# Loading the first piece of w_out as two transfers, of 120 and of 8 partitions, in a packed-attention and feed-forward kernel

## The chip, the cores and the metric

The kernel runs on one core of a Trainium2 chip. The metric is the device time of one execution in microseconds (us). Before the change the median of three runs is 711.92 us (711.51 to 712.25).

## The reference

Each of 8 batches has 8 heads of 576 tokens and 64 dimensions. A set of 32 packed queries `p` attends to `k` and `v`, and the queries `q` attend to what comes out; the heads of a token, side by side, are the 512 inputs of a feed-forward layer with 2048 hidden units.

```
p_packed = sm_attn(p, k, v)
out = sm_attn(q, p_packed, p_packed)
x = attn_out.transpose(0, 2, 1, 3).reshape(B * S, H * D)
h = x @ w_in
g = np.maximum(h, 0.0) + alpha * np.minimum(h, 0.0)
return (g @ w_out)
```

`w_in` (512 x 2048) and `w_out` (2048 x 512) come as 64-bit floats and are turned into 32-bit ones on the chip.

## The kernel before

The second attention is not multiplied out: the kernel multiplies the packed result with `w_in` first (`packed_w`, tiles `pw`), and TensorE (PE) then forms the hidden units of a tile of tokens from the attention weights and `pw` (`first`, lines 764 to 812) and from them the output (`second`, lines 878 to 921, and `row_second`). A tile has 288 or 256 tokens, a step of the main loop one tile and one of 16 blocks of hidden units. The first four tiles are swept over a part of the hidden units at a time, so that the weights can arrive and be converted meanwhile.

Before the main loop lies a start of some 25 us in which batch 0 goes through its whole attention. Its order is a string of letters, `go("inaaauoiaaaIaboaiiaa0abooavbawaOIx")` (line 990): `a` and `b` take a step of the attention of batch 0 and 1, `i` and `o` load the next piece of `w_in` and `w_out`, `I` and `O` convert one, `u`, `v`, `w`, `x` issue spare matmuls (`keep_busy`). The instructions of each engine run in the order that a scheduler settled when the kernel was built.

`w_out` is loaded in eight pieces (`w_out_load`, line 202). Piece `g` is 256 rows of 512 64-bit numbers, two rows for each of 128 partitions, 1 MB in one DMA. All loads go through `load` (line 181), and nearly all are issued by SyncE (SP) at line 189, in the order in which the program asks for them.

The framework gives each DMA one of eight semaphores in turn, `DMAHW0` to `DMAHW7`. Before SP issues a DMA it waits until the DMA that had the same semaphore before, the eighth before it, has landed. So at most eight are under way. Whoever reads the data waits for that semaphore too.

The first piece (tile `wraw0`, in the profile `wraw<-in_w_out`) is converted by `to_half` (line 153): ScalarE (ACT) takes the magnitude of the upper words (line 151, to `wo_whole`), then the sign and the lower words (lines 175 and 176, to `rest`); VectorE (DVE) limits and shifts the magnitude (lines 166 and 169) and adds `rest` (line 177). Right behind it ACT converts the second piece of `w_in` (`wraw5`, again lines 151 and 131), on which DVE waits with line 132. The first product with `w_out` is at line 896.

Of the kernel before, what the change touches and what calls it, by code (L numbers as in the profile page):

```python
# [27 lines left out]
def pack_attention_ffn_kernel(  # L28
# [19 lines left out]
    B, NP, P, S = qT.shape  # L48
# [132 lines left out]
    def load(out, in_, eng=None):  # L181

        if eng is not None:
            other.append(eng.dma_start(out=out, in_=in_))
            return
        with ExitStack() as behind:
            if queue:
                behind.enter_context(tc.issue_after(queue[-1].ins))
            ins = nc.sync.dma_start(out=out, in_=in_)
        if written:  # L190
            queue[:] = [ins]

    first_half, begun = [], []
    last_mm, queue, written, raws, tail, whole, w0, other = [], [], [True], {}, {}, [], [], []
# [6 lines left out]

    def w_out_load(g):
        raws["o", g] = const.tile([P, 2, 512], U64, name=f"wraw{g}", tag=f"wo{g}")
        load(raws["o", g], w_out[2 * g * P : 2 * (g + 1) * P, :].rearrange("(a p) d -> p a d", p=P))

    def w_out_convert(g):
        if g < QF:
# [747 lines left out]
    def go(what):  # L955


        for ch in what:
            if ch in BUSY:
                keep_busy(BUSY[ch], values[BEHIND[ch]] if ch in BEHIND else None)  # L960
            elif ch == "n":
                load(al, alpha)
                nc.gpsimd.tensor_scalar(
                    out=nal, in0=al, scalar1=-1.0, scalar2=1.0, op0=ALU.mult, op1=ALU.add
                )
            elif ch in "ab":
                next(a0 if ch == "a" else a1, None)
            elif ch in counts:
                n = counts[ch]
                counts[ch] += 1  # L970
                if ch == "0":
                    if n < 2:
                        packed_w(0, 0, (n,))
                    else:
                        packed_w(0, n - 1)
                elif ch == "1":
                    packed_w(1, n, (None,) if n else (0, 1))
                else:
                    with ExitStack() as behind:
                        for ins in tail.values() if ch != "A" else []:  # L980
                            behind.enter_context(tc.issue_after(ins.ins))
                        {
                            "i": w_in_load, "I": w_in_convert, "o": w_out_load,
                            "O": w_out_convert, "S": w_out_late_split, "H": late_a, "A": w_out_begin,
                        }[ch](n)
# [142 lines left out]
```

## Time and profile before

| | before |
|---|---|
| median of 3 runs | 711.92 us (711.51 to 712.25) |
| the profiled execution: time / span | 712.62 us / 710.8 us |
| busy: PE, DVE, ACT | 98%, 67%, 50% of the span |
| DMA | 85.36 MB, mean 120 GB/s |
| DMA from 0 to 60 us | 21.12 MB, mean 352 GB/s |

The span runs from the first to the last instruction; the execution's time has some 2 us around it. The profile names a group of instructions by its line, engine, operation and tiles (written <- read). All times inside an execution are us from the start of the span.

### The profile page before, as it was taken

Reading aid. Unit: us, or ns where it says so; the run is one execution under the profiler, and the core shown is the slowest. Engines: PE = TensorE matmul, PEld = TensorE weight load, DVE = VectorE, ACT = ScalarE, POOL = GpSimd, SP = SyncE. Lnnn points to the kernel's source line nnn. Section 1 sums busy time; section 2 is a strip of 40 time slices with the busy share of each in tenths; the row PEclk is TensorE's granted clock in tenths of the full one; section 3 lists DMA queues with packets and bytes.
Section 4 is the critical chain, followed back from the end, with each engine's and each line's share of the span. In section 5 each row is a group of like instructions: output and inputs, shape, how many; then the busy total and the mean of one; then the engine's idle time right before and its main releaser. Section 6 shows DMA issues by size and latency. Waiting matters only on the chain.

```text
span 710.8 us, 14597 instructions
## 1 busy us (share of the span) xinstructions
PE 695.5 (98%) x5600; PEld 599.2 (84%) x5600; DVE 474.3 (67%) x1067; ACT 358.1 (50%) x846; POOL 33.0 (5%) x128
## 2 busy tenths in 40 slices
PE   6899999999999999999999999999999999999997
PEld 3578998899898888888878888888887888798897
DVE  4999888865796568656773567846694456964443
ACT  3796788944355535444443454545353333533232
POOL 1001200001001200001000010001000000000000
PEclk9899999999999999999999999999999999999999
DMA  9996474133534422452323423334314203010100
GB/s 312 385 342 244 129 261 151 60 104 122 155 117 156 135 59 99 148 156 73 126 47 118 156 68 127 125 100 120 97 59 152 66 7 95 25 30 1 30 16 30
DMA packets 77188, 85.36 MB, mean 120 GB/s; under 512 B 34880, under 2 KB 57920, under 8 KB 77120
## 3 DMA queue, kind: packets, MB, share of 16 engines
q1 hardware_dynamic: 76480, 83.89, 36.4%
q8 instruction: 44, 0.72, 0.4%
q10 hardware_dynamic: 640, 0.56, 0.2%
q14 instruction: 24, 0.20, 0.1%
HBM read 70.79 MB, written 13.63 MB: 119 GB/s over the span
## 4 chain that ended last, share of the span: by engine, by line
PE 92%; DVE 3%; DMA 2%; ACT 2%; issue 0%; SPq 0%; DVEq 0%
PE acc L832 40%; PE ps_h L780 9%; PE ps_h L782 9%; PE ps_h L781 9%; PE acc L899 5%; PE acc L900 5%; PE acc L901 5%; PE ps_m L375 4%; PE ps_j L375 3%; PE acc L896 2%; PE acc L375 2%; DMA wraw<-in_w_out 1%; DMA xtwo<-in_kT 1%; PE ps_h L774 1%; PE spare L286 0%
## 5 line engine op out<-in xcount | busy, mean ns | idle before, releaser
L832 PE MATMUL acc<-wo,gh 128*128 128x512 f32 x704 | 200.1, 398 | 0.0
L787 ACT ACTIVATE neg<-ps_h 128x256 f32<-128x256 f32 (+2 forms) x256 | 105.4, 412 | 164.4 <-PE ps_h L782 157.8
L801 DVE SCALAR_TENSOR_TENSOR neg<-neg,nal,ps_h 128x256 f32<-128x256 f32 (+1 forms) x248 | 119.6, 483 | 77.1 <-ACT neg L787 76.6
L811 ACT CAST gh<-neg 128x256 fp32r<-128x256 f32 (+1 forms) x248 | 101.7, 411 | 111.3 <-DVE neg L801 110.0
L780 PE MATMUL ps_h<-a_h,pw 128*128 128x256 f32 (+2 forms) x496 | 146.4, 295 | 0.8 <-DVE neg L801 0.8
L782 PE MATMUL ps_h<-a_h,pw 128*128 128x256 f32 (+2 forms) x496 | 146.6, 296 | 0.0
L781 PE MATMUL ps_h<-a_l,pw 128*128 128x256 f32 (+2 forms) x496 | 146.5, 295 | 0.0
L812 DVE TENSOR_TENSOR gl<-neg,gh 128x256 fp32r<-128x256 f32 (+1 forms) x248 | 104.4, 425 | 61.5 <-ACT gh L811 59.8
L832 PEld LDWEIGHTS acc<-wo,gh 128*128 128x128 f32 x704 | 126.7, 195 | 21.9 <-issue 4.2
L832 PE MATMUL acc<-wo,gl 128*128 128x512 f32 x352 | 115.5, 394 | 0.0
L780 PEld LDWEIGHTS ps_h<-a_h,pw 128*128 128x128 f32 x496 | 93.5, 188 | 7.6 <-DVE neg L801 1.3
L781 PEld LDWEIGHTS ps_h<-a_l,pw 128*128 128x128 f32 x496 | 93.4, 188 | 7.2
L782 PEld LDWEIGHTS ps_h<-a_h,pw 128*128 128x128 f32 x496 | 93.5, 189 | 0.1
L900 PE MATMUL acc<-gh,wo 128*128 128x288 f32 (+1 forms) x280 | 79.7, 293 | 0.5 <-DVE wo L237 0.5
L832 PEld LDWEIGHTS acc<-wo,gl 128*128 128x128 f32 x352 | 68.7, 195 | 13.5
L899 PE MATMUL acc<-gh,wo 128*128 128x288 f32 (+1 forms) x280 | 80.0, 296 | 0.0
L901 PE MATMUL acc<-gl,wo 128*128 128x288 f32 (+1 forms) x280 | 69.8, 293 | 0.0
L899 PEld LDWEIGHTS acc<-gh,wo 128*128 128x128 f32 x280 | 52.6, 189 | 5.0 <-ACT pw L730 3.4
L900 PEld LDWEIGHTS acc<-gh,wo 128*128 128x128 f32 x280 | 52.8, 189 | 0.7 <-DVE wo L237 0.7
L794 DVE SCALAR_TENSOR_TENSOR rest<-neg,nal,ps_h 128x64 f32<-128x64 f32 x96 | 26.6, 277 | 40.1 <-ACT neg L787 40.1
L901 PEld LDWEIGHTS acc<-gl,wo 128*128 128x128 f32 x280 | 48.6, 188 | 0.7 <-issue 0.5
L832 PE MATMUL acc<-wo,rparts 128*128 128x512 f32 x144 | 35.3, 397 | 0.0
(157 smaller groups left out, 690.1 us busy)
## 6 DMA issues: line engine op xcount, KB each, us to landing
w<-w_whole SPq DMA_DIRECT2D x48, 512.0 KB, 5.8
wraw<-in_w_in SPq DMA_DIRECT2D x8, 1024.0 KB, 10.9
wraw<-in_w_out SPq DMA_DIRECT2D x8, 1024.0 KB, 6.8
xraw<-in_kT SPq DMA_DIRECT2D x28, 288.0 KB, 4.5
xraw<-in_qT SPq DMA_DIRECT2D x28, 288.0 KB, 4.6
vraw<-in_v SPq DMA_DIRECT2D x96, 64.0 KB, 2.1
outT<-out SPq DMA_DIRECT2D x44, 128.0 KB, 2.2
w_whole<-w SPq DMA_DIRECT2D x6, 512.0 KB, 7.6
```

The costliest lines, as they stand in the source:

```text
L375: mm = nc.tensor.matmul(out, lhs, rhs, start=start, stop=stop)
L780: nc.tensor.matmul(x, w[:, 0, i], a_h[:, i], start=(i == 0), stop=False)
L781: nc.tensor.matmul(x, w[:, 0, i], a_l[:, i], start=False, stop=False)
L782: mm = nc.tensor.matmul(x, w[:, 1, i], a_h[:, i], start=False, stop=(i == 1))
L787: marks[:] = [mm, nc.scalar.activation(out=neg, in_=x, func=AF.Relu, scale=-1.0)]
L801: nc.vector.scalar_tensor_tensor(out=g, in0=neg, scalar=nal[:, f : f + 1], in1=x, op0=ALU.mult, op1=ALU.add)
L811: late[:] = [nc.scalar.copy(out=gh, in_=g)]
L812: nc.vector.tensor_tensor(out=gl, in0=g, in1=fv(gh), op=ALU.subtract)
L832: mm = nc.tensor.matmul(ps, g, wo_t[f][:, part_], start=(f == 0 and i == 0), stop=(f == NF - 1 and i == 2))
L899: nc.tensor.matmul(ps, wo_t[f][:, 0, os_], gh, start=begin, stop=False)
L900: nc.tensor.matmul(ps, wo_t[f][:, 1, os_], gh, start=False, stop=False)
L901: mm = nc.tensor.matmul(ps, wo_t[f][:, 0, os_], gl, start=False, stop=end)
```

## The change

`w_out_load` issues the load of piece 0 as two DMAs into the same tile: partitions 0 to 119 and partitions 120 to 127. The other seven pieces stay one DMA each.

```diff
     def w_out_load(g):
         raws["o", g] = const.tile([P, 2, 512], U64, name=f"wraw{g}", tag=f"wo{g}")
-        load(raws["o", g], w_out[2 * g * P : 2 * (g + 1) * P, :].rearrange("(a p) d -> p a d", p=P))
+        src = w_out[2 * g * P : 2 * (g + 1) * P, :].rearrange("(a p) d -> p a d", p=P)
+        for part_ in ((slice(0, 120), slice(120, P)) if g == 0 else (slice(0, P),)):
+            load(raws["o", g][part_], src[part_])
```

SP has one DMA more, and every later DMA gets the next semaphore of the eight. On SP, from the last two loads of `q` for batch 0 (`xtwo`) on, there stands before the change (`wraw4`, `wraw5`, `wraw6` are pieces of `w_in`, `xraw` is `k` of batch 1):

```order
L189 DMA xtwo_130<-in_qT 128x2x288 [waits DMAHW5_49]
L189 DMA xtwo_131<-in_qT 128x2x288 [waits DMAHW6_49]
L189 DMA wraw0_178<-in_w_out 128x2x512 [waits DMAHW7_49,PE_49]
L189 DMA wraw5_180<-in_w_in 128x4x256 [waits DMAHW0_49]
L189 DMA praw_226<-in_pT 128x128 [waits DMAHW1_49]
L189 DMA xraw_228<-in_kT 128x576 [waits DMAHW2_49]
L189 DMA xraw_230<-in_kT 128x576 [waits DMAHW3_49]
L189 DMA xraw_232<-in_kT 128x576 [waits DMAHW4_49]
L189 DMA xraw_234<-in_kT 128x576 [waits DMAHW5_49]
L189 DMA wraw1_236<-in_w_out 128x2x512 [waits DMAHW6_49,PE_49]
L189 DMA wraw6_283<-in_w_in 128x2x512 [waits DMAHW7_49]
L189 DMA wraw4_285<-in_w_in 128x2x512 [waits DMAHW0_49,DVE_49,Activation_49]
```

and with the change, at the same place of SP:

```order
L189 DMA xtwo_131<-in_qT 128x2x288 [waits DMAHW6_49]
L189 DMA wraw0_178<-in_w_out 120x2x512 [waits DMAHW7_49,PE_49]
L189 DMA wraw0_178<-in_w_out 8x2x512 [waits DMAHW0_49]
L189 DMA wraw5_181<-in_w_in 128x4x256 [waits DMAHW1_49]
L189 DMA praw_227<-in_pT 128x128 [waits DMAHW2_49]
L189 DMA xraw_229<-in_kT 128x576 [waits DMAHW3_49]
L189 DMA xraw_231<-in_kT 128x576 [waits DMAHW4_49]
L189 DMA xraw_233<-in_kT 128x576 [waits DMAHW5_49]
L189 DMA xraw_235<-in_kT 128x576 [waits DMAHW6_49]
L189 DMA wraw1_237<-in_w_out 128x2x512 [waits DMAHW7_49,PE_49]
L189 DMA wraw6_284<-in_w_in 128x2x512 [waits DMAHW0_49]
L189 DMA wraw4_286<-in_w_in 128x2x512 [waits DMAHW1_49,DVE_49,Activation_49]
```

From `wraw5` to the second piece of `w_out` (`wraw1`), seven loads now wait for a DMA that is one later in the program than before: `wraw1` waited for the last load of `q` and now waits for the 120 partitions of `wraw0`. From `wraw6` on each load waits for the DMA it waited for before (where that was `wraw0`, for the 8 partitions).

On ACT, at the conversion of the first piece, before:

```order
L551 ACTIVATE t1_291<-t1_291 128x576 [waits DVE_49]
L151 ACTIVATE wo_whole_376<-wraw0_178 128x1024 [waits DMAHW7_49]
L175 ACTIVATE rest_377<-wraw0_178,tiny_106 128x1024 [waits Activation_49]
L176 ACTIVATE rest_377<-wraw0_178 128x1024 [waits Activation_49]
L151 ACTIVATE w_384<-wraw5_180 128x1024 [waits DMAHW0_49]
```

and with the change (lines behind 205 are two higher):

```order
L553 ACTIVATE t1_292<-t1_292 128x576 [waits DVE_49]
L151 ACTIVATE wo_whole_377<-wraw0_178 128x1024 [waits DMAHW7_49,DMAHW0_49]
L175 ACTIVATE rest_378<-wraw0_178,tiny_106 128x1024 [waits Activation_49]
L176 ACTIVATE rest_378<-wraw0_178 128x1024 [waits Activation_49]
L151 ACTIVATE w_385<-wraw5_181 128x1024 [waits DMAHW1_49]
```

The instruction at line 151 waits for both DMAs; the order of ACT, DVE and PE is as it was.

## Rows read from the trace of the kernel before

**Rows 1.** The page: busy time of the engines, share of the span, instructions.

```profile
PE   695.5 (98%) x5600; PEld 599.2 (84%) x5600; DVE 474.3 (67%) x1067; ACT 358.1 (50%) x846; POOL 33.0 (5%) x128
```

**Rows 2.** Waits for a DMA, whole span: total, times, longest (us).

```profile
PE acc L375 <- DMA xtwo<-in_kT: 4.6, 2, 4.2
...
ACT wo_whole L151 <- DMA wraw<-in_w_out: 0.5, 1, 0.5
```

**Rows 3.** The chain that ended last, 0 to 40 us: start, length, work.

```profile
11.70 8.98 DMA wraw<-in_w_out
...
20.70 1.12 ACT wo_whole L151
...
25.34 0.69 DVE w L132
```

**Rows 4.** Timeline of ACT: start, length, instruction, idle before and its releaser.

```profile
19.55 0.68 ACT L551 ACTIVATE t<-t 128x576 f32<-128x576 f32 x1 [0.82 <-DVE t L541]
20.70 1.12 ACT L151 ACTIVATE wo_whole<-wraw 128x1024 f32<-128x1024 f32 x1 [0.47 <-DMA wraw<-in_w_out]
...
29.32 1.15 ACT L151 ACTIVATE wo_whole<-wraw 128x1024 f32<-128x1024 f32 x1
```

**Rows 5.** Waits of DVE from 20 to 60 us, all of them.

```profile
DVE w L132 <- ACT w L151: 0.9, 1, 0.9
```

**Rows 6.** DMA issues from 0 to 11.69 us: count, KB each, median us to landing.

```profile
xtwo<-in_qT SPq DMA_DIRECT2D x4, 288.0 KB, 7.5
wraw<-in_w_in SPq DMA_DIRECT2D x1, 1024.0 KB, 7.3
vtwo<-in_v SPq DMA_DIRECT2D x2, 512.0 KB, 8.6
xtwo<-in_kT SPq DMA_DIRECT2D x3, 288.0 KB, 4.5
xtwo<-in_kT ACTq DMA_DIRECT2D x1, 288.0 KB, 4.1
vtwo<-in_v SPq DMA_DIRECT2D x2, 64.0 KB, 8.2
praw<-in_pT ACTq DMA_DIRECT2D x1, 64.0 KB, 2.7
```

**Rows 7.** Stretches: length, busy time (instructions) of each engine, granted clock, DMA share, GB/s.

```profile
0.00:4.00 4.00, 0.00 (x0) 0.00 (x0) 0.00 (x0) 1.49 (x2) 1.80 (x13) 1.00 0.48 154
4.00:8.00 4.00, 3.44 (x32) 0.65 (x32) 0.82 (x2) 0.00 (x0) 0.00 (x0) 1.00 1.06 372
8.00:12.00 4.00, 4.00 (x27) 3.95 (x24) 2.12 (x9) 2.78 (x9) 0.20 (x1) 1.00 1.03 330
12.00:16.00 4.00, 2.15 (x84) 1.47 (x82) 3.75 (x7) 1.85 (x6) 0.00 (x0) 1.00 1.09 348
16.00:18.00 2.00, 1.94 (x48) 0.81 (x48) 1.97 (x4) 0.00 (x1) 0.00 (x0) 1.00 1.04 415
18.00:20.00 2.00, 1.23 (x10) 1.19 (x10) 1.97 (x4) 1.11 (x3) 0.00 (x0) 1.00 1.02 382
...
24.00:28.00 4.00, 4.00 (x24) 1.97 (x23) 3.10 (x5) 2.91 (x5) 0.00 (x0) 0.53 1.03 409
```

**Rows 8.** DMA queues, 14 to 18 us: packets, MB, share of 16 engines.

```profile
q8 instruction: 1, 0.02, 1.6%
```

**Rows 9.** DMA issued from 16.8 to 17 us: the second piece of w_out.

```profile
wraw<-in_w_out SPq DMA_DIRECT2D x1, 1024.0 KB, 12.3
```

**Rows 10.** Timeline of SP: start, length of the issue.

```profile
2.29 0.47 SPq L189 DMA_DIRECT2D wraw<-in_w_in  x1
...
12.11 0.47 SPq L189 DMA_DIRECT2D wraw<-in_w_in  x1
13.62 0.34 SPq L189 DMA_DIRECT2D praw<-in_pT  x1
...
16.87 0.38 SPq L189 DMA_DIRECT2D wraw<-in_w_out  x1
```

## The prediction

> **What bounds the kernel now.** I began with the page: PE is busy for 695.5 of the 710.8 us [rows 1], so at most 15.3 us of the span can be won anywhere without taking work from PE. The change touches a load, so the second view was the waits for a DMA over the whole span [rows 2]. The reader is to see how few there are: PE waits for the first `k` at the very start, and the only wait for `w_out` is one of 0.5 us on ACT, at line 151. Third came the chain that ended last [rows 3]: it runs through the first piece of `w_out`, from its issue at 11.70 to line 151 at 20.70, on ACT to the magnitude of the next piece, and from there to DVE at 25.34. The timeline of ACT [rows 4] gives the wait its size: line 551 ended at 19.55 + 0.68 = 20.23, and ACT then sat idle for 0.47 us. Last, the waits of DVE [rows 5]: between 20 and 60 us it waits once worth listing, 0.9 us, for the magnitude that ACT makes. So what ACT loses at 20.2 DVE loses at 25.3, and after that DVE is the engine that PE waits for.
>
> **Why that load lands late.** The bytes asked for up to the first `w_out` piece are the issues of [rows 6] (4 x 288 + 1024 + 2 x 512 + 4 x 288 + 2 x 64 + 64 = 4544 KB, the 8 KB of `alpha` left out) and its own 1024 KB: 5568 KB, or 5.70 MB. What moved, by stretch [rows 7]: 4 x (154 + 372 + 330 + 348) GB/s = 4.82 MB by 16 us, 0.83 MB more by 18, and 382 GB/s from there. So 5.70 MB had moved at 18.1 us, and the piece landed at 20.7. If the 16 DMA engines were level, the time between would be the tail of a transfer. For the first `w_in` piece the same sum gives 2.29 MB (2240 KB), reached at 8.6, with its landing at 2.29 + 7.3 = 9.6 [rows 6, 10]: a tail of 1.0. For `w_out` it is 2.5, so some 1.5 us are something else. One thing in these microseconds is out of the ordinary: a single instruction packet of 16 KB that took 1.6% of 16 engines over 4 us, 0.016 x 16 x 4 = 1.02 us [rows 8]. Being one packet, it occupied one engine. My reading is that one DMA engine falls a good 1 us behind, and that a transfer dealt over all 16 waits for it.
>
> **The change, part by part.**
> - *The split.* Dealt evenly, each of 16 engines carries 8 partitions of the piece, 64 KB. At 382 / 16 = 23.9 GB/s [rows 7] a partition of 8 KB costs an engine 0.34 us. How 120 partitions are dealt no row shows, since all loads here have a multiple of 16. I take 15 engines with 8 each, because 120 is 15 x 8, and one partition each on eight engines for the rest: one engine then carries nothing, eight carry nine.
> - *If the late engine is the one left out*, the piece lands at 18.1 + 1.0 + 0.34 = 19.5, before ACT is free at 20.23. Line 151 starts at 20.25, 0.45 us earlier. More cannot come, since ACT's earlier work is not moved. DVE's 0.9 us shrinks by the same 0.45, and everything behind it in the start moves up by that. What is late next is ACT itself.
> - *If it is not left out*, it is among the other 15 and the landing stays at 20.7, or is 0.34 later if it is one of the eight with a ninth partition.
> - *One more issue on SP*, 0.4 us like the others (0.34 to 0.47 [rows 10]), and seven loads that wait for a DMA one place later. The `w_in` piece goes from 12.11 to 13.6, where the DMA behind it stood, whose wait it takes over [rows 10]; the second `w_out` piece from 16.87 to the landing of the first, 19.5 to 21.0. Cost: nothing, as long as work lies ahead of them. Asked for by then are 5.70 + 1024 + 64 + 4 x 288 KB = 8.0 MB, moved by 20.7 are 5.64 + 2.7 x 0.38 = 6.7. The 1.3 MB between are 3.4 us of DMA time, more than the shortest time to landing in the start, 2.7 us [rows 6]. The second piece used to land at 16.87 + 12.3 = 29.2 [rows 9] and is read at 29.32 [rows 4]; with this cover it still does. If the cover were gone, the gap of some 2 us would pass on to it, and ACT at 29.3 would be late by as much.
> - *A second semaphore on line 151*: no row prices it on ACT; between nothing and 0.1 us, I take nothing.
>
> Sum: 0.45 us less, in the profiled execution 712.62 - 0.45 = 712.17. The median lies 0.70 below that execution, so 711.92 - 0.45 = **711.5 us**. That is 0.06%, and about 0.2% (1.4 us) is what a measurement of this kernel can tell from no change: the verdict should be "same".
>
> [...]
>
> **The rivals.**
> - *The late engine is not left out*: 711.9, or 712.3 if it takes a ninth partition. For it: no row numbers the engines. [...]
> - *Fewer engines, slower.* 120 is no multiple of 16, and if it is dealt to 8 engines, each carries 15 partitions instead of 8: 7 x 0.34 = 2.4 us more, landing at 23.1. ACT, DVE and all behind them are late by 2.4: 714.3. It turns the change over once the late engine carries more than its 8 partitions of now, and can be measured from four more on (4 x 0.34 = 1.4 us). Nothing in the trace speaks for it.
> [...]
>
> **How the numbers follow.** Late engine left out, 711.5: 0.45, a choice and not a count, since blind odds would be far lower and a fixed place at the end of the row is what lifts them. Not left out: 0.28 for 712.3 and 0.13 for 711.9. Fewer engines: 0.05. Clock better 0.05, worse 0.04. The runs before spread by -0.4 and +0.3, so 711.5 to 712.3 with that spread is 711.1 to 712.6; with a little for the clock on either side the range is 710.8 to 712.9, which leaves out the fewer engines and most of the clock cases. Below 710.5 lies the better clock: faster 0.05. Above 713.3 lie fewer engines and the worse clock: slower 0.09. Same: 0.86.
>
> **What would show it.** Right: two issues of `w_out` near 11.7 and 12.1, the second piece of `w_out` issued at 19 to 20 instead of 16.87, ACT's line 151 at 20.25 with no wait for a DMA, DVE's wait at line 132 near 0.45, the start of DVE's and PE's later work 0.4 to 0.45 earlier. Wrong: line 151 at 20.7 or 21.0 with the second `w_out` issue just before it (the late engine still carries the piece), or at 23 (fewer engines); a wait of ACT at its second line 151 near 29.3 (the cover was gone); the granted clock low in a stretch where it was full.

## The result and the profile after

| | before | after |
|---|---|---|
| median of 6 runs each, side by side | 712.17 us (711.51 to 712.95) | 716.05 us (715.33 to 717.3) |
| the profiled execution: time / span | 712.62 / 710.8 us | 715.46 / 713.6 us |
| ratio, 95% interval | | 1.0053 [1.0042, 1.0063] |

The change costs 3.9 us by the medians and 2.8 in the two profiled executions, of which the one after lies 0.6 below its median and the one before 0.45 above its own. The prediction was 711.5, within [710.8, 712.9]: wrong, and on the wrong side.

Lines behind 205 are two higher than in the rows of before. The page, first the busy time of the engines, which answers to [rows 1], and its row of the loads' DMA queue:

```profile
PE 697.2 (98%) x5600; PEld 598.9 (84%) x5600; DVE 474.9 (67%) x1067; ACT 357.9 (50%) x846; POOL 32.8 (5%) x128
...
q1 hardware_dynamic: 76487, 83.89, 36.9%
```

No engine does more work to speak of. The queue has 76,487 packets for the same 83.89 MB. Before it had 76,480, so there are 7 more, to which x2_64_64 below comes back:

```profile
q1 hardware_dynamic: 76480, 83.89, 36.4%
```

The chain that ended last, which answers to [rows 3], start, length, work:

```profile
11.84 11.47 DMA wraw<-in_w_out
...
23.37 9.30 DMA wraw<-in_w_out
32.66 0.02 issue
32.69 0.02 ACT wo_whole L151
```

The first piece now lands at 11.84 + 11.47 = 23.3, where it landed at 20.7; behind it the chain runs through a second load of `w_out`. The timeline of ACT, which answers to [rows 4] (start, length, instruction, idle before and its releaser):

```profile
20.29 0.69 ACT L553 ACTIVATE t<-t 128x576 f32<-128x576 f32 x1
23.39 1.15 ACT L151 ACTIVATE wo_whole<-wraw 128x1024 f32<-128x1024 f32 x1 [2.41 <-DMA wraw<-in_w_out]
...
32.69 1.16 ACT L151 ACTIVATE wo_whole<-wraw 128x1024 f32<-128x1024 f32 x1 [0.48 <-DMA wraw<-in_w_out]
```

ACT waits 2.41 us for the piece where it waited 0.47, and its line 151 starts at 23.39, 2.69 later. DVE inherits that (waits of DVE from 20 to 60 us, against [rows 5]):

```profile
DVE w L132 <- ACT w L151: 2.1, 1, 2.1
```

DVE's line 132 moved from 25.34 to 28.04 (2.70), its transpose of batch 0's last attention weights (line 568, now 570) from 37.08 to 39.79 (2.71), and the span grew by 2.8. So the loss is complete at line 151 and travels through unchanged. The chain runs through the second load as well, but DVE has no idle time left between 28.04 and 39.79, so the wait for that load adds nothing. Where it arises is seen in the stretches, with the columns of [rows 7]; first the kernel after:

```profile
16.00:20.00 4.00, 2.60 (x51) 1.34 (x52) 3.93 (x7) 0.36 (x2) 0.00 (x0) 1.00 1.04 201
20.00:24.00 4.00, 2.61 (x21) 2.23 (x21) 2.89 (x6) 1.59 (x4) 0.00 (x0) 1.00 1.02 240
24.00:28.00 4.00, 3.28 (x12) 1.45 (x12) 1.39 (x2) 3.97 (x5) 0.00 (x0) 0.52 1.06 388
28.00:32.00 4.00, 4.00 (x19) 1.90 (x15) 3.96 (x6) 2.24 (x6) 0.00 (x0) 0.63 1.03 406
```

and the same stretches before:

```profile
16.00:20.00 4.00, 3.16 (x58) 2.00 (x58) 3.93 (x7) 1.12 (x4) 0.00 (x0) 1.00 1.03 398
20.00:24.00 4.00, 2.58 (x13) 2.42 (x12) 3.83 (x8) 3.50 (x4) 0.00 (x0) 0.61 1.06 385
```

This is the main reading. The DMA engines are as busy as before (share 1.04 against 1.03; the share adds up the time of all packets, and can come out above 1), and move half as much: 201 GB/s against 398. They lack nothing to do; what they do takes longer. The granted clock is no cause: before it is 0.61 and 0.53 from 20 to 28 us [rows 7 for the second], after it is 0.52 and 0.63 from 24 to 32 (the last two rows of after), the same low stretch some 4 us later; and x2_64_64 below, with a granted clock of 1.00 from 16 to 32 us, is as slow. One microsecond of it by packets, 16 to 17 us, after:

```profile
DMA packets 55, 0.19 MB, mean 186 GB/s; under 512 B 0, under 2 KB 10, under 8 KB 55
## 3 DMA queue, kind: packets, MB, share of 16 engines
q1 hardware_dynamic: 55, 0.19, 105.4%
```

and before:

```profile
DMA packets 117, 0.44 MB, mean 436 GB/s; under 512 B 4, under 2 KB 13, under 8 KB 117
## 3 DMA queue, kind: packets, MB, share of 16 engines
q1 hardware_dynamic: 117, 0.44, 108.4%
```

The share times 16 engines and 1 us, divided by the packets, is the mean time of one: 1.054 x 16 / 55 = 0.31 us after, 1.084 x 16 / 117 = 0.15 before. A packet takes twice as long.

### The profile page after: what moved, and what is told of

Read it like the earlier page. It is cut to its first block, busy times and chain, and to the rows that moved or that the text cites. A ratio compares the mean times of both kernels' runs of the same rounds, so it can differ in the third digit from the quotient of the medians.

```text
span 713.6 us, 14600 instructions
## 1 busy us (share of the span) xinstructions
PE 697.2 (98%) x5600; PEld 598.9 (84%) x5600; DVE 474.9 (67%) x1067; ACT 357.9 (50%) x846; POOL 32.8 (5%) x128
## 2 busy tenths in 40 slices
DMA packets 77195, 85.36 MB, mean 120 GB/s; under 512 B 34887, under 2 KB 57927, under 8 KB 77127
## 3 DMA queue, kind: packets, MB, share of 16 engines
q1 hardware_dynamic: 76487, 83.89, 36.9%
## 4 chain that ended last, share of the span: by engine, by line
PE 89%; DMA 5%; DVE 3%; ACT 2%; issue 1%; SPq 0%; DVEq 0%
PE acc L834 40%; PE ps_h L782 9%; PE ps_h L784 9%; PE ps_h L783 9%; PE acc L901 5%; PE acc L902 5%; PE acc L903 5%; PE ps_m L377 3%; DMA wraw<-in_w_out 3%; PE ps_j L377 3%; PE acc L377 2%; DMA wraw<-in_w_in 1%; DMA xtwo<-in_kT 1%; DVE wo L239 0%; PE spare L288 0%
```

## The experiments

Theories: **A**, a transfer over part of the partitions is slow by itself, whatever else is under way: its packets take longer, and by how much depends on which partitions it covers. Why it should be so, no run shows. Against it stood: one more DMA (its issue, its semaphore, the later waits of SP); that only 15 engines carry the large part; that the rows are read from memory in a worse order; that other traffic of the start is in the way.

| run | first piece cut into | time us | ratio [95%] | GB/s, 16 to 20 us | ACT L151 at |
|---|---|---|---|---|---|
| before | whole | 712.17 | 1 | 398 | 20.70 |
| after | 120 + 8 partitions | 716.05 | 1.0053 [1.0042, 1.0063] | 201 | 23.39 |
| x1_two_rows | two rows, 128 partitions each | 712.29 | 0.9994 [0.9985, 1.0003] | 395 | 20.23 |
| x2_64_64 | 64 + 64 partitions | 716.39 | 1.0049 [1.0034, 1.0063] | 210 | 23.89 |
| x3_112_16 | 112 + 16 partitions | 715.09 | 1.003 [1.0017, 1.0043] | 252 | 23.45 |
| x4_source_order | 120 + 8, other source rows | 717.6 | 1.0059 [1.0042, 1.0076] | 193 | 26.17 |
| y2_columns | 480 + 32 columns, 128 partitions | 712.39 | 1.0001 [0.9991, 1.001] | 381 | 20.58 |
| y3_96_32 | 96 + 32 partitions | 714.07 | 1.0026 [1.0016, 1.0035] | 225 | 21.81 |
| z3_mid_first | 32..95, 0..31, 96..127 | 714.17 | 1.0017 [1.0007, 1.0027] | 256 | 20.95 |

Each ratio is to runs of the kernel before on the same chip, with medians of 712.97 (x runs), 712.26 (y), 712.68 (z1, z2) and 712.81 (z3).

**Two transfers, all partitions** (x1_two_rows). The piece's two rows are the two DMAs, 512 KB each (this cut and those of y2 and z3 are shown against the changed kernel):

```diff
-        for part_ in ((slice(0, 120), slice(120, P)) if g == 0 else (slice(0, P),)):
-            load(raws["o", g][part_], src[part_])
+        for part_ in ((slice(0, 1), slice(1, 2)) if g == 0 else (slice(0, 2),)):
+            load(raws["o", g][:, part_], src[:, part_])
```

> The first piece of w_out is loaded as two transfers of all 128 partitions, one per row of a partition (512 KB each), so there is one DMA more and the same shift of the waits on SP as with 120 and 8 partitions, but both are dealt as a whole transfer is. [...] Rival C (one DMA more, the later waits and the second semaphore on ACT cost the time): 715 to 716, the second piece of w_out issued after 20 and landing after 32.

712.29 us, ratio 0.9994 [0.9985, 1.0003]. The DMA from 16 to 17 us, with the columns above:

```profile
DMA packets 128, 0.42 MB, mean 419 GB/s; under 512 B 15, under 2 KB 30, under 8 KB 128
```

and the timeline of ACT:

```profile
20.23 1.11 ACT L151 ACTIVATE wo_whole<-wraw 128x1024 f32<-128x1024 f32 x1
...
28.50 1.15 ACT L151 ACTIVATE wo_whole<-wraw 128x1024 f32<-128x1024 f32 x1 [0.24 <-DMA wraw<-in_w_out]
```

The second DMA, its issue on SP, the second semaphore at line 151 and the seven loads that wait one place later are all here as in the change, and cost nothing that can be measured. The second `w_out` piece was issued at 18.47, and rival C falls. What costs is how the cut goes.

**Half the partitions each** (x2_64_64).

```diff
-        for part_ in ((slice(0, 120), slice(120, P)) if g == 0 else (slice(0, P),)):
+        for part_ in ((slice(0, 64), slice(64, P)) if g == 0 else (slice(0, P),)):
```

> The first piece is loaded as partitions 0 to 63 and 64 to 127. [...] Theory B (15 engines are what is slow): 712 us and 400 GB/s. Rival C: 715 to 716 with 400 GB/s. [...]

716.39 us, as slow as the change with its 716.05; theory B (15 engines) falls. The page's row of the queue, and the stretches:

```profile
q1 hardware_dynamic: 76496, 83.89, 36.8%
```

```profile
16.00:20.00 4.00, 2.16 (x41) 0.79 (x45) 3.78 (x6) 0.27 (x1) 0.00 (x0) 1.00 1.05 210
20.00:24.00 4.00, 2.68 (x35) 2.06 (x21) 3.13 (x7) 1.34 (x4) 0.00 (x0) 1.00 1.01 235
```

76,496 packets are 16 more than before, and all 16 are under 512 B (34,896 such packets against 34,880). x1, whose two DMAs keep all 128 partitions, shows the same two numbers. In the kernel before, SP's 376 DMAs leave 6,016 packets of 4 bytes in the trace, 16 for each DMA, and the page counts 16 engines. The trace numbers no engine; if each engine that takes part leaves one such packet, which is my estimate from these counts, the halves run on as many engines as whole transfers do, and are slow all the same: the engine left idle is not the cause. By the same estimate the change's 7 more, all under 512 B too (34,887), are 15 + 8 in place of 16, that is 15 engines for 120 partitions and 8 for 8.

**112 + 16 and 96 + 32** (x3_112_16, y3_96_32), cut in the same way, with 112 and 96 in place of 64.

> The first piece is loaded as 112 and 16 partitions, 7 and 1 for each of 16 engines. [...] Theory B: 712 us and 400 GB/s. Rival C: 715 to 716.

715.09 us, 252 GB/s from 16 to 20 us, line 151 at 23.45. The queue has 76,496 packets as in x1 and x2, so by that count all 16 engines take part again, and it is still slow.

> The first piece is loaded as 96 and 32 partitions, 6 and 2 for each of 16 engines. Theory A: both transfers cover the partitions unevenly, 250 to 300 GB/s from 16 to 20 us, ACT's line 151 at 22 to 23.5 and 714 to 715.5 us. Theory B (only an odd number of engines is slow): 712 us.

714.07 us, as theory A had it, and 76,496 packets again, but with 225 GB/s from 16 to 20 us (250 to 300 were expected) and 355 from 20 to 24, and with line 151 at 21.81 (22 to 23.5). All four of these cuts across partitions are slower than the whole, and by different amounts; why 96 costs less than 64 was not worked out.

**Another source order** (x4_source_order): 120 + 8 partitions, with the rows of `w_out` read so that a partition's two rows lie side by side in memory. This permutes the rows of `w_out` in the first piece, so the product is with other rows.

```diff
-        src = w_out[2 * g * P : 2 * (g + 1) * P, :].rearrange("(a p) d -> p a d", p=P)
+        src = w_out[2 * g * P : 2 * (g + 1) * P, :].rearrange("(p a) d -> p a d" if g == 0 else "(a p) d -> p a d", p=P)
```

> 120 and 8 partitions as in the change, but partition p takes rows 2p and 2p+1 of the piece instead of rows p and p+128, so that HBM is read in another order while SBUF is written as before. This permutes rows of w_out within the piece, so the output is not the reference's. [...] Rival D (the order in which 15 engines read HBM is what is slow): near 400 GB/s and 712 us.

717.6 us and 193 GB/s: no better with 8 KB read in one run, so the order in which the change reads the rows is not what makes it slow. The loss of 4.6 us by the medians is larger than the change's 3.9, and line 151 comes at 26.17; the piece was issued 1.35 us later than in the change, at 13.19, and why was not followed.

**Cut by columns** (y2_columns): the 960 KB and 64 KB of the change as 480 and 32 of the 512 columns, all 128 partitions.

```diff
-        for part_ in ((slice(0, 120), slice(120, P)) if g == 0 else (slice(0, P),)):
-            load(raws["o", g][part_], src[part_])
+        for part_ in ((slice(0, 480), slice(480, 512)) if g == 0 else (slice(0, 512),)):
+            load(raws["o", g][:, :, part_], src[:, :, part_])
```

> The first piece is loaded as two transfers of all 128 partitions with the same shares of bytes as in the change, 480 of 512 columns and then 32. Theory A: 712 us, 390 to 400 GB/s from 16 to 20 us, ACT's line 151 at 20.2 to 21. Rival F (a long transfer with a short one behind it, or the second wait, is what costs): 714 to 716 us.

712.39 us, ratio 1.0001 [0.9991, 1.001], and 381 GB/s. The same sizes, the same two DMAs, no loss. With x1 this settles that what matters is whether each part keeps all partitions.

**Later pieces** (y1_late_pieces): the first piece whole, three that load after 85 us cut instead.

```diff
+        cuts = {4: (0, 120, P), 5: (0, 64, P), 6: (0, 96, P)}.get(g, (0, P))
+        for lo, hi in zip(cuts, cuts[1:]):
+            load(raws["o", g][lo:hi], src[lo:hi])
```

> The first piece is one DMA again. Three later pieces of w_out, loaded after 85 us when the queues are nearly empty and read long after they land, are split instead: piece 4 as 120 and 8 partitions, piece 5 as 64 and 64, piece 6 as 96 and 32. Theory A: each such transfer is slow by itself, with nothing else under way: the 120 partitions land 6.5 to 7.5 us after their issue (the whole piece took 4.9), those of 64 go at half the rate, and the time stays at 712 us, since nobody waits for these pieces. Rival E (the slow rate comes from other transfers that are under way at the same time): 4.5 to 5 us to landing, 712 us.

712.25 us, ratio 0.9999 [0.9989, 1.0009]. The issues of 85 to 86.2 us, median us to landing, here:

```profile
wraw<-in_w_out SPq DMA_DIRECT2D x1, 960.0 KB, 7.4
```

and before:

```profile
wraw<-in_w_out SPq DMA_DIRECT2D x1, 1024.0 KB, 4.9
```

7.4 us for 960 KB where 1,024 KB took 4.9, and 217 GB/s from 89 to 90 us where before had 410: the cut is slow also away from the traffic of the start, and there it costs no time, because nothing waits for the piece yet.

**Which 64 partitions** (z1_mid_rows, z2_mid_rows_swapped). The halves 0 to 63 and 64 to 127 against the middle 32 to 95, in two late pieces; z2 exchanges 4 and 5.

```diff
+        middle, ends = ((32, 96), (0, 32), (96, P)), ((0, 64), (64, P))
+        for lo, hi in {4: middle, 5: ends}.get(g, ((0, P),)):
+            load(raws["o", g][lo:hi], src[lo:hi])
```

> The first piece of w_out is whole again, so the time is that of the kernel before (712.3) on either theory. In the two pieces that load later with the queue otherwise quiet, the fifth is loaded as partitions 32 to 95 and then the rest, the sixth as partitions 0 to 63 and then 64 to 127. [...] Rival (every transfer of fewer than 128 partitions is slow, whichever they are): the two take the same time to 0.3 us, 4.7 us or more.

> As the run before with the two pieces' cuts exchanged: the fifth piece as partitions 0 to 63 and 64 to 127, the sixth as 32 to 95 and then the rest. Time 712.3 on either theory. Theory A: the 512 KB of partitions 32 to 95 land 3.4 to 4 us after their issue in the sixth piece too, those of 0 to 63 in the fifth at 4.7 us or more, so the difference goes with the partitions and not with the piece. Rival (every transfer of fewer than 128 partitions is slow): no difference that goes with the partitions; both at 4.7 us or more.

712.34 us (0.9993 [0.9982, 1.0004]) and 712.98 (1.0009 [0.9997, 1.002]). Issues at the first of the two pieces, z1, partitions 32 to 95:

```profile
wraw<-in_w_out SPq DMA_DIRECT2D x1, 512.0 KB, 4.5
```

and z2, partitions 0 to 63:

```profile
wraw<-in_w_out SPq DMA_DIRECT2D x1, 512.0 KB, 5.2
```

The difference has the right sign; 4.5 lies above the 3.4 to 4 that theory A expected. While the data flow the two are plain. The queue in z1 from 88 to 89 us, the rest of 32 to 95 and behind it the first of the outer quarters:

```profile
DMA packets 117, 0.41 MB, mean 410 GB/s; under 512 B 17, under 2 KB 17, under 8 KB 117
## 3 DMA queue, kind: packets, MB, share of 16 engines
q1 hardware_dynamic: 117, 0.41, 110.5%
```

and in z2 from 89 to 90 us, 0 to 63 and then 64 to 127 under way:

```profile
DMA packets 61, 0.22 MB, mean 217 GB/s; under 512 B 8, under 2 KB 8, under 8 KB 61
## 3 DMA queue, kind: packets, MB, share of 16 engines
q1 hardware_dynamic: 61, 0.22, 111.0%
```

1.105 x 16 / 117 = 0.15 us a packet against 1.11 x 16 / 61 = 0.29. The same number of partitions and bytes on the same queue, and the middle runs at the full rate. In z1 the remaining quarters, 0 to 31 and 96 to 127, then run at 229 GB/s (89 to 90 us). At the second of the two pieces the landings say less (5.9 us for 0 to 63 in z1, 5.1 for the middle in z2), because slow parts of the piece before lay ahead of both. The rates there are as clear, with the pieces exchanged. In z2 from 94 to 95 us, 32 to 95 alone:

```profile
DMA packets 103, 0.40 MB, mean 397 GB/s; under 512 B 6, under 2 KB 6, under 8 KB 103
```

and in z1 from 93.25 to 94.25 us, 0 to 63 and then 64 to 127:

```profile
DMA packets 58, 0.20 MB, mean 201 GB/s; under 512 B 9, under 2 KB 9, under 8 KB 58
```

The rival that any transfer of fewer than 128 partitions is slow falls. Two things stay open. The first half microsecond of 0 to 63 runs at the full rate too (393 GB/s in z2 from 88.25 to 88.75 us), and why the slow rate sets in only then is not shown. And other partitions are also other rows of `w_out`; no run loads the middle from the rows of a half, so that partitions and not rows decide rests on x4, where another order of the rows did not help.

Side by side, the middle ran at 397 and 410 GB/s, the halves at 201 and 217, and the whole piece of the kernel before at 398. Why the time of a packet depends on the partitions, for the 120 too, no run shows.

**The middle in the changed piece** (z3_mid_first).

```diff
-        for part_ in ((slice(0, 120), slice(120, P)) if g == 0 else (slice(0, P),)):
-            load(raws["o", g][part_], src[part_])
+        for lo, hi in ((32, 96), (0, 32), (96, P)) if g == 0 else ((0, P),):
+            load(raws["o", g][lo:hi], src[lo:hi])
```

> The first piece of w_out again, now as three transfers: partitions 32 to 95 (512 KB), 0 to 31 and 96 to 127 (256 KB each). Cut in half as 0 to 63 and 64 to 127 it cost 3.5 us (716.4 against 712.9), some 1.75 us for each half that runs at half speed. [...] Rival (any transfer of fewer than 128 partitions is slow, and each more one adds to it): +3.5 us or more, line 151 at 23.9 or later, about 210 GB/s from 16 to 20 us.

714.17 us, ratio 1.0017 [1.0007, 1.0027], 256 GB/s: +1.4 us where the halves cost 3.4, with one DMA more. If only the outer parts, half of the bytes, are slow, half of the 3.4, 1.7 us, should be lost by that estimate. The rate falls where the outer parts follow the middle, with a granted clock of 1.00 in both stretches:

```profile
16.00:17.00 1.00, 1.00 (x32) 0.41 (x16) 0.94 (x1) 0.00 (x0) 0.00 (x0) 1.00 1.11 394
17.00:18.00 1.00, 0.81 (x20) 0.21 (x16) 1.00 (x3) 0.00 (x0) 0.00 (x0) 1.00 1.06 176
```

Line 151 starts at 20.95 with a wait of 0.61, and the second piece is waited for too (timeline of ACT):

```profile
30.25 1.19 ACT L151 ACTIVATE wo_whole<-wraw 128x1024 f32<-128x1024 f32 x1 [1.26 <-DMA wraw<-in_w_out]
```

The profiled execution (713.05) is the fastest of the ten, so it shows less than the median's loss.

**Is there a late engine?** (y4_fetch_later). The kernel before, with one spare matmul in place of seven in `u`, so that the packet of 16 KB of [rows 8] comes later.

```diff
-    BUSY = {"u": 7, "v": 4, "w": 2, "x": 3, "y": 3, "z": 2}
+    BUSY = {"u": 1, "v": 4, "w": 2, "x": 3, "y": 3, "z": 2}
```

> The kernel before, with one spare matmul instead of seven at the first u of the start, so that PE's instruction stream is shorter by 24 instructions and the 16 KB instruction packet comes later; the spare matmuls compute nothing that is used. The theory of the prediction (this packet holds up one DMA engine and with it the first piece): with the packet after 19 us the piece lands by 20, ACT's line 151 starts at 20.2 to 20.3 without a wait, and the time is 711.5 to 712.5 beside 712 (unless the granted clock falls in a stretch where it was full). Rival: the piece lands at 20.7 as before, and the packet has nothing to do with it.

714.55 us, ratio 1.0024 [1.0015, 1.0034]. The packet lies between 18 and 20 us now. The issue of the piece at 12.43:

```profile
wraw<-in_w_out SPq DMA_DIRECT2D x1, 1024.0 KB, 7.7
```

7.7 us to landing, where before it was 9.0. By itself that says little: fewer spare matmuls move everything else too (ACT reaches line 151 at 21.82, and the kernel is 1.7 us slower by the ratio, for reasons that were not followed), and in y1, z1 and z2, where the piece is whole and the packet comes at 17 to 18 us, the piece landed 8.6, 7.9 and 7.6 us after its issue.

The packets in the traces, one by one, say more. In the kernel before, first the instruction packet (the stretch from 17.28 to 17.30 us), then a packet that starts some 15 ns before that one ends (18.312 to 18.314):

```profile
q8 instruction: 1, 0.02, 322.2%
...
q1 hardware_dynamic: 1, 0.00, 1378.1%
```

3.222 x 16 x 0.02 = 1.03 us, from 17.30 to 18.33, and then 13.781 x 16 x 0.002 = 0.44 us for 4 KB, which otherwise take 0.16. Each of the 13 traces has a packet that starts 13 to 15 ns before this instruction packet ends, and it takes 0.44 us where it has 4 KB (eight traces), 0.41 where it has 3,840 B (y2) and 0.23 where it has 2 KB (four). I read it as the next packet of the same engine. Behind the instruction packet, so read, that engine still had eight packets of the piece in the kernel before, five in y1, two in z1, none in z2 and y4, and the piece landed 9.0, 8.6, 7.9, 7.6 and 7.7 us after its issue. In the kernel before, the last of them ended at 20.12, and the last of any other engine at 18.88. By this reading there is a late engine, the instruction packet makes it late, and the piece is late only as far as that engine still has packets of it to carry. The wait of 0.47 us that the prediction wanted to win hangs on that: y1, z1 and z2 start line 151 at 20.87, 20.24 and 21.03 without a wait for the piece, y1 and z2 also because ACT comes later there.

With the change the instruction packet runs from 19.52 to 20.88 (first row, the stretch from 19.50 to 19.55 us), and the packet behind it is the second row (20.86 to 20.87):

```profile
q8 instruction: 1, 0.02, 170.2%
...
q1 hardware_dynamic: 1, 0.00, 275.6%
```

Again 0.44 us and 4 KB, and at that time only the first piece of `w_out` moves in packets of 4 KB. So by this reading the late engine was not the one that the 120 partitions left out.

## Why the prediction was wrong

**The step that failed is "The split".** It kept the rate: "At 382 / 16 = 23.9 GB/s a partition of 8 KB costs an engine 0.34 us", however the partitions are dealt. The count agrees with the 7 packets, by the estimate above 15 engines and 8; the rate was wrong. At 201 GB/s the engines carry 12.6 each, and with twice the time, the 8 partitions that an engine of the 15 carries cost 8 x 0.34 = 2.7 us more. Measured is a landing at 23.3 instead of 20.7, 2.6 later, and instead of the 19.5 forecast. I had no row of a transfer over 120 partitions, and bounded its cost by the number of partitions an engine carries alone; that a packet might take longer had no bound at all. What is shown is that the rate depends on which partitions a part covers (397 GB/s for 32 to 95, 201 to 217 for the halves); the reason is not shown.

**The late engine** decided the sign of the forecast and carried 0.45 of the chance. By the reading of the packets above it exists: in the kernel before, it ended 1.2 us behind the others at this landing (20.12 against 18.88), where the prediction had 1.5 from sums over stretches. But the choice that this engine is the one left out rested on a fixed place at the end of the row, which no run shows, and with the change that engine still carried a 4 KB packet of the piece. So by that reading this branch would not have held in this execution at the full rate either. And the gain was one execution's: three others with the whole piece have no such wait.

**The rival "fewer engines"** had the side, and its 2.4 us are near the 2.8 of the profiled executions (its 714.3 is below the median of 716.05), at a chance of 0.05. That was luck: x2 is as slow with all 16 engines at work, by the estimate from its packets, so fewer engines are not the cause.

**One more issue, the semaphores and the waits of SP**: right that they cost nothing (x1, y2). The second `w_out` piece was issued at 23.37, not at 19.5 to 21.0, because it waits for the late first. ACT then waits 0.48 us for it at 32.69, but y1, whose second piece is issued at 16.81 as before, shows such a wait too (0.24), and DVE's delay is no longer behind it than ahead (2.70, 2.71). The cover held. The chances given to the clock, 0.05 and 0.04, rest on no run: with the 0.53 of 24 to 28 us [rows 7], a start at 1.00 would by my estimate win at most 4.0 x (1 - 0.53) = 1.9 us, but x1 and y2 have a granted clock of 1.00 from 16 to 32 us and take 712.00 and 712.50 us in their profiled executions, not 1.9 less than 712.62.

**A part not foreseen**: the slow transfers also hold up the loads around them. PE's weight load for the packed attention waited 0.2 us for the last load of `q` and now waits 1.8 (waits from 12 to 24 us, before and after):

```profile
PEld acc L375 <- DMA xtwo<-in_qT: 0.2, 1, 0.2
...
PEld acc L377 <- DMA xtwo<-in_qT: 1.8, 1, 1.8
```

That load is issued ahead of the piece and is still under way when the piece's packets start. x2 and x4 have such waits too, of 1.7 and 1.6 us; x1, y1, y2, z1 and z2 have 0.2 at most. ACT's line 553 ends at 20.98, where it ended at 20.23, but this is not shown to follow from it: y1 and z2, with the piece whole, end the line at 20.96 and 21.12. What it does show is that "ACT's earlier work is not moved" was not safe: it varies by more than the 0.45 us that the prediction wanted to win.

## What to carry to other kernels

Before a load is cut, ask which partitions each part covers, not only how many bytes or engines: parts that keep all 128 partitions (by rows or by columns) were free here (395 and 381 GB/s where the whole piece had 398), cuts across the partitions ran at half to two thirds of the rate (193 to 256), with one exception, partitions 32 to 95 (397). In the profile such a transfer showed as a full DMA share (1.04) with half the GB/s (201), and the time of one packet, share x engines x time / packets (0.31 us against 0.15), is the number to compare. It cost time only where something waited for the piece: the same cuts later in the kernel cost nothing (y1, ratio 0.9999). And before a wait of half a microsecond is priced, look whether another execution has it.

## What was not expected of the hardware

- 64 partitions are not like any other 64: 0 to 63 with 64 to 127 behind them ran at 201 to 217 GB/s, 32 to 95 at 397, on the same queue.
- A transfer over 120 partitions left the DMA share at 1.04 while the rate fell from 398 to 201 GB/s: the busy share didn't tell that packets took longer (0.31 us against 0.15).
- The slow transfer held back loads issued ahead of it (1.8 us of wait for `q` in place of 0.2).
- One instruction packet of 16 KB took 1.03 us, and by my reading held one DMA engine for that time: the load landed 9.0 us after its issue where that engine still had eight packets of it to carry, and 7.6 and 7.7 where it had none.

No version tried is faster than the kernel before; x1 and y2 equal it.
